# Statistics of the first rows split another way over ScalarE and VectorE, one-column matmuls alternating with q heads, and a flag read in mid FFN

## The chip, the cores and the metric

One core of one Trainium2 chip. The metric is device time in microseconds (us) of one execution. Each timed run also reports the span from the first to the last instruction and the mean granted TensorE clock, to three digits.

## The reference, cut to what matters

```python
h1 = layernorm(x) * (1 + scale_a) + shift_a      # scale, shift, gates = 6 pieces of silu(c) @ w_mod
q  = h1 @ wq                                     # 32 heads of 128
x  = x + gate_a * (windowed_attention(q, k_cache, v_cache) @ wo)
h2 = layernorm(x) * (1 + scale_b) + shift_b
out = x + gate_b * ((silu(h2 @ w_gate) * (h2 @ w_up)) @ w_down)
```

2048 rows of 1024 columns, bf16, a feed-forward network (FFN) 3584 wide. A flag, computed on the chip from bounds on q and k, selects a general attention path; with these inputs it is 0, and the general path is jumped over.

## The kernel before

Rows go in four blocks of 512. For the first block the modulation is folded into the q heads. The normalised rows are transposed into PSUM (`h0_ps`) and multiplied by 1 + scale (`hs`). Seven heads are computed from `hs`, and the shift's part of q is added later as a bias per head (`bias_q`). That bias comes out of matmuls which stream a single column: `mod_cols` computes scale and shift, 8 matmuls for each 128 of them, and `shift_cols` computes shift times wq, 28 matmuls for each half.

```python
    def stats_0(t):                      # VectorE: mean and variance of row tile t
        mv = ln[t] = sm.tile(...)
        ln_stats(t, mv)
        rstd_0(t)                        # ScalarE: 1/sqrt(variance)
    stats_0(0); act_sum(3); stats_0(1)   # act_sum, act_squares: the same statistics on ScalarE
    xpose_0(0, ln_norm(0)); warm(4)      # warm(n): n useless matmuls of 512 columns
    act_squares(3); stats_0(2); rstd_0(3, 1.0 / D)
    xpose_0(1, ln_norm(1)); warm(4)
    # ... (cut) ...
    nc.scalar.activation(out=hs[0][:, 0, :], in_=h0_ps[0][:, 0, :], ..., scale=ca1[:, 0:1])
    nc.vector.tensor_copy(out=h10[:, 0:2, :], in_=h0_ps[0][:, 0:2, :])   # rows kept for later heads
    h_scale(1)                                                           # hs from h10, on VectorE
    nc.vector.tensor_copy(out=h10[:, 2:4, :], in_=h0_ps[0][:, 2:4, :])
    h_scale(2); h_scale(3)
    # ... (cut: first halves, dt 0 to 3, of all seven heads) ...
    for g in range(4):
        q0(g, range(4, DT))              # second half of head g: 4 matmuls of 512 columns
    sa_cols(0)                           # 32 one-column matmuls (shift, first half)
    q0(4, range(4, DT))
    for dt in range(4):
        ln_mod(("h1", 0), dt, ca1, sa)
    shift_cols(0)                        # 28 one-column matmuls, then bias_q on VectorE
    sa_cols(1)                           # 32
    q0(5, range(4, DT))
    shift_cols(1)                        # 28
    q0(6, range(4, DT))
```

## Time and profile before

| | before |
|---|---|
| median of the first three runs (low to high) | 1274.93 us (1273.68 to 1275.57) |
| the profiled run, its span and mean clock | 1273.63 us, 1271.9 us, 1.000 |
| TensorE (PE) busy | 1262.7 us, 99% |
| PE idle before 31 us / from 31 us to the last matmul / after it | 3.84 / 0.18 / 5.19 us |

The prediction shows the lines that carry this: the busy times by stretch, PE's timeline of the start, the chain, and the flag's instructions at the end. One more view is needed, VectorE's timeline of the first 10 us (start us, busy us, engine, line, operation, out<-in, count, and in brackets the idle time ahead of it and what ended it). Row tile x2 had landed at 5.58, x3 at 6.24.

```profile
6.77 1.28 DVE L833 BATCH_NORM_STATS2 st<-x 128x6 f32<-128x512 bf16 x2
...
9.65 1.00 DVE L852 TENSOR_SCALAR xn<-x,mv 128x1024 bf16<-128x1024 bf16 x2 [0.95 <-ACT mv L954]
```

VectorE comes to x2 at 6.77 without a wait. The last two row tiles are normalised from 9.65 on, and what they wait for is ScalarE (ACT), which makes the statistics of x3.

### The profile page before, as it was taken

To read this page: it belongs to the slowest core of one execution; us is meant where nothing else is said; L and a number is where in the kernel's file an instruction comes from. 1 tells how busy PE (TensorE), PEld (TensorE's weight loads), DVE (VectorE), ACT (ScalarE), POOL (GpSimd) and SP (SyncE) were. 2 spreads that over 40 slices of the span, in tenths; PEclk is the share of its full clock that TensorE was granted. 3 is DMA by queue.
4 is the path that set the end of the run, shared out by engine and by line. 5 is a ranking of instruction groups with operands and counts; after the bars stand their busy time and mean duration, and the time that the engine had idled before them with its cause. 6 is when DMAs were issued, how large, how long until landed. Compare 5 with 4: busy or idle time off the path is not lost.

```text
span 1271.9 us, 18166 instructions
## 1 busy us (share of the span) xinstructions
PE 1262.7 (99%) x7587; PEld 641.2 (50%) x7587; DVE 609.0 (48%) x1335; ACT 334.9 (26%) x439; POOL 1.3 (0%) x10
## 2 busy tenths in 40 slices
PE   8999999999999999999999999999999999999998
PEld 4555555555555555555554444444444444444444
DVE  4766568977587756476664632311222112221122
ACT  3543334443343433334341111011100111011100
POOL 0000000000000000000000000000000000000000
PEclk9999999999999999999999999999999999999999
DMA  9897657768556655455575466536633565425701
GB/s 290 203 246 180 175 133 176 170 171 195 142 134 173 152 137 153 113 154 112 120 203 145 135 224 184 161 96 212 210 116 102 171 213 179 157 91 172 242 22 64
DMA packets 306844, 204.46 MB, mean 161 GB/s; under 512 B 145601, under 2 KB 303297, under 8 KB 306754
## 3 DMA queue, kind: packets, MB, share of 16 engines
q1 hardware_dynamic: 301842, 199.03, 57.7%
q10 hardware_dynamic: 4912, 4.20, 1.0%
q8 instruction: 61, 1.00, 0.3%
q14 instruction: 29, 0.24, 0.1%
HBM read 165.94 MB, written 4.21 MB: 134 GB/s over the span
## 4 chain that ended last, share of the span: by engine, by line
PE 98%; DVE 1%; DMA 0%; issue 0%; ACT 0%; ACTq 0%
PE gu_ps L1299 30%; PE a_ps L1217 17%; PE q_ps L1142 16%; PE d_ps L1319 15%; PE o_ps L1185 9%; PE s_ps L1153 9%; PE q_ps L1013 1%; DVE st L833 0%; DVE junk L1076 0%; PE mod_ps L773 0%; DMA x<-in_A_x_dram 0%; PE h_ps L948 0%; DVE qT L934 0%; DVE hT L873 0%; DVE junk L804 0%
## 5 line engine op out<-in xcount | busy, mean ns | idle before, releaser
L1155 ACT ACTIVATE pT<-s_ps 128x1024 bf16<-128x1024 f32 x256 | 249.2, 1021 | 346.8 <-PE s_ps L1153 346.8
L1217 PE MATMUL a_ps<-wo,oT 128*128 128x512 bf16 x1024 | 241.9, 379 | 0.0
L1142 PE MATMUL q_ps<-hT,wq 128*128 128x512 bf16 x968 | 229.2, 379 | 0.0
L1305 DVE TENSOR_TENSOR guT<-gu_ps,sg 128x512 bf16<-128x512 f32 x112 | 77.4, 692 | 284.4 <-ACT sg L1304 284.4
L1299 PE MATMUL gu_ps<-hT,wg 128*128 128x512 bf16 x896 | 211.7, 379 | 0.0
L1304 ACT ACTIVATE sg<-gu_ps 128x512 bf16<-128x512 f32 x112 | 66.9, 597 | 488.6 <-PE gu_ps L1299 480.1
L1319 PE MATMUL d_ps<-wd,guT 128*128 128x512 bf16 (+2 forms) x952 | 194.2, 366 | 0.0
L1299 PE MATMUL gu_ps<-hT,wu 128*128 128x512 bf16 x672 | 163.3, 379 | 0.0
L1217 PEld LDWEIGHTS <-oT 128*128 128x128 bf16 x1024 | 100.2, 98 | 120.6
L934 DVE CAST qT<-q_ps 128x512 bf16<-128x512 f32 x121 | 83.6, 691 | 147.9 <-PE q_ps L1142 147.6
L1142 PEld LDWEIGHTS <-wq 128*128 128x128 bf16 x968 | 94.7, 98 | 114.1
L1319 PEld LDWEIGHTS <-guT 128*128 128x128 bf16 x952 | 90.9, 98 | 103.0
L1185 PEld LDWEIGHTS <-pT 128*128 128x128 bf16 x2048 | 126.7, 98 | 30.8 <-issue 0.4
L1299 PEld LDWEIGHTS <-wg 128*128 128x128 bf16 x896 | 87.6, 98 | 105.5
L1185 PE MATMUL o_ps<-v_sb,pT 128*128 128x130 bf16 x2048 | 137.1, 220 | 0.1
L1153 PE MATMUL s_ps<-qT,kT 128*128 128x512 bf16 x512 | 131.9, 379 | 0.1
L1299 PEld LDWEIGHTS <-wu 128*128 128x128 bf16 x672 | 65.8, 98 | 79.3
L1172 DVE TENSOR_TENSOR oq<-o_ps,rl 128x256 bf16<-128x256 f32 (+2 forms) x256 | 100.5, 419 | 3.7
L1323 DVE TENSOR_TENSOR f<-d_ps,gb_bc 128x512 f32<-128x512 f32 (+2 forms) x34 | 22.5, 660 | 140.5 <-PE d_ps L1319 140.5
L1225 DVE TENSOR_TENSOR acc<-a_ps,acc 128x512 f32<-128x512 f32 x64 | 44.1, 689 | 37.2 <-PE a_ps L1217 37.2
L1153 PEld LDWEIGHTS <-kT 128*128 128x128 bf16 x512 | 44.9, 98 | 30.8 <-issue 0.5
L1299 PE MATMUL gu_ps<-hT,v_sb 128*128 128x512 bf16 x224 | 57.5, 379 | 0.0
(92 smaller groups left out, 420.7 us busy)
## 6 DMA issues: line engine op xcount, KB each, us to landing
wq<-in_A_wq_dram SPq DMA_DIRECT2D x64, 512.0 KB
wo<-in_A_wo_dram SPq DMA_DIRECT2D x64, 512.0 KB
wg<-in_B_w_gate_dram SPq DMA_DIRECT2D x56, 512.0 KB
wd<-in_B_w_down_dram SPq DMA_DIRECT2D x56, 512.0 KB
wu<-in_B_w_up_dram SPq DMA_DIRECT2D x42, 512.0 KB
v_sb<-in_B_w_up_dram SPq DMA_DIRECT2D x14, 512.0 KB
x<-in_A_x_dram SPq DMA_DIRECT2D x16, 256.0 KB
wm<-in_w_mod_dram SPq DMA_DIRECT2D x4, 1024.0 KB
```

The lines of the kernel that those rows point to most:

```text
L934: nc.vector.tensor_copy(out=t, in_=q_ps)
L1142: nc.tensor.matmul(q_ps, lhsT=w, rhs=hT[("h1", cc)][:, dt, :], start=(dt == 0), stop=(dt == DT - 1))
L1153: nc.tensor.matmul(s_ps[:, i, :], lhsT=kT[:, kv, j * P:(j + 1) * P], rhs=qT[g], start=True, stop=True)
L1155: nc.scalar.activation(out=p[:, 2 * jj:2 * jj + 2, :], in_=s_ps, func=ACT.Exp, scale=scale)
L1172: nc.vector.tensor_tensor(out=dst, in0=ps[:, s0:s0 + cnt, 0:Dh], in1=sc, op=ALU.mult)
L1185: nc.tensor.matmul(o_slot["ps"][:, s_, :], lhsT=pT[g][:, j, t * P:(t + 1) * P], rhs=v_sb[:, kv, j, 0:VN], start=(j == 0), stop=(j == WT - 1))
L1217: nc.tensor.matmul(a_ps, lhsT=oT[(cc, 2 * q + i)][:, hh % 4, t * P:(t + 1) * P], rhs=wo_tiles[(cc, q, dh, i)][:, hh % 4, :], start=(hh == ...
L1225: nc.vector.tensor_tensor(out=acc[(cc, t)][:, dsl], in0=a_ps, in1=acc[(cc, t)][:, dsl], op=ALU.add)
L1299: nc.tensor.matmul(ps[:, n, :], lhsT=gu_w[(cc, fg, nm, dt // 4)][:, dt % 4, fi * P:(fi + 1) * P], rhs=hT[("h2", cc)][:, dt, :], start=(dt ...
L1304: nc.scalar.activation(out=g, in_=ps[:, 0, :], func=ACT.Silu)
L1305: nc.vector.tensor_tensor(out=guT[(cc, fg)][:, fi, :], in0=ps[:, 1, :], in1=g, op=ALU.mult)
L1319: nc.tensor.matmul(d_ps, lhsT=guT[(cc, f // 4)][:, f % 4, t * P:(t + 1) * P], rhs=wd_tiles[(cc, dh, f // 4)][:, f % 4, c0:c0 + w], start=( ...
```

## The change

The intent: share the statistics so that neither engine waits for the other, scale the first row blocks straight out of PSUM on both engines, put a head between any two groups of one-column matmuls, and read the flag on each engine in the second FFN block in place of the end.

```diff
     stats_0(0)
-    act_sum(3)
-    stats_0(1)
+    act_sum(1)
+    rstd_0(0)
+    stats_0(2)
+    act_squares(1)
+    warm(3)
     xpose_0(0, ln_norm(0))
     ... (cut: warm(5), stats_0(3), xpose_0 of 1, 2 and 3)
+    h_scale(0, h0_ps[0][:, 0, :])              # VectorE, out of PSUM
     ... (cut: a modulation group)
+    h_scale(1, h0_ps[0][:, 1, :], True)        # ScalarE
     ... (cut: two modulation groups)
+    h_scale(2, h0_ps[0][:, 2, :])
+    h_scale(3, h0_ps[0][:, 3, :], True)
+    for dt in (0, 2):
+        nc.vector.tensor_copy(out=h10[:, dt:dt + 2, :], in_=h0_ps[0][:, dt:dt + 2, :])
     ... (cut)
     shift_cols(0)
+    q0(5, range(4, DT))
     sa_cols(1)
-    q0(5, range(4, DT))
+    q0(6, range(4, DT))
     shift_cols(1)
-    q0(6, range(4, DT))
     ... (cut)
     for cc in range(NTC):                      # FFN blocks
+        if cc == 1:
+            over = nc.values_load(flag[0:1, 0:1], min_val=0, max_val=1)
     ... (cut: a dependency that keeps each engine but PE from moving its read to the end)
-        over = nc.values_load(flag[0:1, 0:1], min_val=0, max_val=1)
         with tc.If(over > 0):
             general_path(tc, *args)
```

More of the change, by code (lines that the diff above doesn't have):

```diff
@@ L958, in stats_0 @@
         ln_stats(t, mv)
-        rstd_0(t)
     def act_sum(t):
@@ L973, in fast_path, with h_scale @@
     stats_0(0)
-    act_sum(3)
-    stats_0(1)
+    act_sum(1)
[3 more added lines that the diff above has]
+    warm(3)
     xpose_0(0, ln_norm(0))
-    warm(4)
-    act_squares(3)
-    stats_0(2)
-    rstd_0(3, 1.0 / D)
+    rstd_0(1, 1.0 / D)
+    rstd_0(2)
+    warm(5)
+    stats_0(3)
     xpose_0(1, ln_norm(1))
-    warm(4)
-    n2 = ln_norm(2)
+    xpose_0(2, ln_norm(2))
+    rstd_0(3)
     n3 = ln_norm(3)
     mod_cols(1, 0, ca1, True, (0,))
-    xpose_0(2, n2)
     xpose_0(3, n3)
-    mod_cols(1, 0, ca1, True, (1, 2, 3))
     hT[("h1", 0)] = h10
     hs = [blkA("hs", [P, 4, TCW]) for _ in range(DH)]
-    def h_scale(dt):
-        nc.vector.tensor_scalar(out=hs[dt // 4][:, dt % 4, :], in0=h10[:, dt, :],
-                                scalar1=ca1[:, dt:dt + 1], scalar2=None, op0=ALU.mult)
-    nc.scalar.activation(out=hs[0][:, 0, :], in_=h0_ps[0][:, 0, :], func=ACT.Identity,
-                         scale=ca1[:, 0:1])
-    nc.vector.tensor_copy(out=h10[:, 0:2, :], in_=h0_ps[0][:, 0:2, :])
-    h_scale(1)
-    nc.vector.tensor_copy(out=h10[:, 2:4, :], in_=h0_ps[0][:, 2:4, :])
-    h_scale(2)
-    h_scale(3)
+    def h_scale(dt, src=None, on_act=False):
+        src = h10[:, dt, :] if src is None else src
+        if on_act:
+            nc.scalar.activation(out=hs[dt // 4][:, dt % 4, :], in_=src, func=ACT.Identity,
+                                 scale=ca1[:, dt:dt + 1])
+        else:
+            nc.vector.tensor_scalar(out=hs[dt // 4][:, dt % 4, :], in0=src,
+                                    scalar1=ca1[:, dt:dt + 1], scalar2=None, op0=ALU.mult)
+    h_scale(0, h0_ps[0][:, 0, :])
+    mod_cols(1, 0, ca1, True, (1,))
+    h_scale(1, h0_ps[0][:, 1, :], True)
+    mod_cols(1, 0, ca1, True, (2, 3))
+    h_scale(2, h0_ps[0][:, 2, :])
+    h_scale(3, h0_ps[0][:, 3, :], True)
+    for dt in (0, 2):
+        nc.vector.tensor_copy(out=h10[:, dt:dt + 2, :], in_=h0_ps[0][:, dt:dt + 2, :])
     nc.scalar.copy(out=h10[:, 4:8, :], in_=h0_ps[1])
@@ L1348, in fast_path @@
     for cc in range(NTC):
+        if cc == 1:
+            at_load = len(nc.cur_bb.bb.instructions)
+            over = nc.values_load(flag[0:1, 0:1], min_val=0, max_val=1)
         for fg in range(NFG):
@@ L1369, in fast_path @@
     assert not tasks
+    loads = {}
+    for ins in nc.cur_bb.bb.instructions[at_load:]:
+        if ins.engine not in loads:
+            loads[ins.engine] = ins.name
+        elif loads[ins.engine] and ins.engine != mybir.EngineType.PE:
+            tc.add_manual_dep(
+                ins, loads[ins.engine],
+                mybir.DependencyInfo(mybir.DependencyClass.NoSync, mybir.DependencyReason.DATA),
+                reason="flag is read before the end")
+            loads[ins.engine] = None
+    return over
 def kernel(tc, *args):
@@ L1375 @@
         flag = gp.tile([1, 1], I32, name="flag")
-        fast_path(tc, flag, *args)
-        over = nc.values_load(flag[0:1, 0:1], min_val=0, max_val=1)
+        over = fast_path(tc, flag, *args)
         with tc.If(over > 0):
```

## The prediction

> **What bounds the kernel now.** I began with the page's busy table: TensorE (PE) is busy 1262.7 of 1271.9 us at full granted clock, so the change can only touch the 9.2 us in which it is not. The busy times by stretch say where those are.
>
> ```profile
> core 0: us, PE busy (x) PEld busy (x) DVE busy (x) ACT busy (x) POOL busy (x), PEclk, DMA share, GB/s
> 0.00:1.60 1.60, 0.00 (x1) 0.10 (x1) 0.66 (x3) 0.85 (x1) 0.70 (x6) 1.00 0.00 0
> 1.60:12.70 11.10, 9.83 (x86) 4.89 (x86) 6.90 (x16) 7.11 (x20) 0.60 (x4) 1.00 0.97 319
> 12.70:31.00 18.30, 17.33 (x213) 9.81 (x213) 7.44 (x26) 2.60 (x4) 0.00 (x0) 1.00 1.12 294
> 31.00:1266.70 1235.70, 1235.52 (x7290) 626.39 (x7287) 593.39 (x1291) 324.33 (x417) 0.00 (x0) 1.00 0.58 158
> 1266.70:1271.90 5.20, 0.00 (x0) 0.00 (x0) 0.58 (x2) 0.00 (x0) 0.00 (x0) 1.00 0.10 24
> ```
>
> From 31 us to the last matmul PE idles 0.18 us in all. What can be won lies in the first 31 us (the normalisation of the first 512 rows and the first seven q heads) and in the last 5.2 us. PE's timeline of the start then shows each of its waits:
>
> ```profile
> 11.89 0.81 PE L1013 MATMUL q_ps<-hs,wq 128*128 128x512 bf16 x3
> 13.16 0.81 PE L1013 MATMUL q_ps<-hs,wq 128*128 128x512 bf16 x3 [0.47 <-DVE hs L993]
> 14.15 3.18 PE L1013 MATMUL q_ps<-hs,wq 128*128 128x512 bf16 x14 [0.18 <-DVE hs L993]
> ...
> 23.15 0.94 PE L773 MATMUL mod_ps<-siluc,wm 128*128 128x1 bf16 x32
> ...
> 25.91 0.94 PE L773 MATMUL mod_ps<-siluc,wm 128*128 128x1 bf16 x32 [0.26 <-DVE bias_q L1027]
> ```
>
> The first heads wait for scaled rows (hs), and later a group of one-column matmuls waits until VectorE has emptied their PSUM buffer. The chain that ended last goes on from there:
>
> ```profile
> 27.73 0.69 PE sh_ps L1024 x28
> 28.43 0.02 issue
> 28.45 0.18 DVE bias_q L1029
> 28.63 0.03 issue
> 28.65 0.76 DVE qT L938
> 29.41 0.02 issue
> 29.43 0.02 ACTq L936
> 29.45 0.04 issue
> 29.50 0.70 ACT qT L936
> 30.19 0.04 issue
> 30.24 0.59 PE s_ps L1153 x2
> ```
>
> The first score matmul (s_ps) is bound by the last shift columns (sh_ps), by way of the bias add and two q evacuations in a row: 30.24 - 28.25 (the last shift column's start) = 1.99 us. From s_ps on PE is full, so the start is worth what s_ps moves.
>
> At the end, the instructions of the flag's line and of the branch's line:
>
> ```profile
> L1377 DVEq TENSOR_LOAD <-flag x1: 540/540/540, 1267.0 to 1267.0; - x1
> L1377 ACTq TENSOR_LOAD <-flag x1: 474/474/474, 1267.7 to 1267.7; - x1
> ...
> L1378 ACTq COMPARE_BRANCH  x1: 54/54/54, 1268.3 to 1268.3; - x1
> ```
>
> After that branch ScalarE's next instruction comes at 1270.90, and SyncE's closing waits end 0.05 us after it; VectorE's branch is at 1267.7 and its next instruction at 1270.7.
>
> [...] 2.6 us from branch to next instruction on ScalarE, 3.0 on VectorE. The change leaves the branches where they are. [...] the 128x1024 bf16 PSUM copy took 0.69 us, the 128x512 fp32 one 0.69 too. [...] ScalarE's first q evacuation (29.50) waits for VectorE's (to 29.40) [...]. In the built program the new scaling has such waits: row block 2 on VectorE waits for block 1 on ScalarE, block 3 on ScalarE for block 2.
>
> **The change part by part.**
>
> 1. Statistics. ScalarE takes x1, not x3; VectorE does x0, x2, x3. The x tiles land at 3.49, 4.13, 5.58 and 6.24. VectorE: stats of x0 from 3.52 (1.3 + 0.2 as now), then idle until x2 at 5.61 (before, x1 followed at 4.97); aggregate 6.92, xn0 7.05, stats of x3 7.46 to 8.98, xn1 8.90, xn2 9.36. ScalarE: sum of x1 4.65 to 5.70, rstd0 to 6.23, squares 6.36 to 7.6, rstd1 to 8.2, rstd2 to 8.6, rstd3 9.01 to 9.54. So xn3 starts at about 9.82, against 10.11 now: 0.29 us. The 0.95 us idle on VectorE in front of xn2 goes, but 0.64 us comes back as the wait for x2.
>
> 2. Scaling. Transposes of block 3 start at 10.56 (now 10.72), so hs0 can start at 10.99. On VectorE from PSUM, at the copy's rate: 0.16 + 512 x 0.52 ns = 0.43 us (estimate). Then modT1 11.38, hs1 on ScalarE 11.6 to 12.3 (0.69 each, as now), hs2 on VectorE 12.33 to 12.77, hs3 on ScalarE 12.81 to 13.5. The heads follow: hs0 at 11.64 (behind the modulation matmuls), hs1 12.34, hs2 12.98 (now 14.15), hs3 13.63 to 14.27. By that alone PE is 1.17 us early.
>
> 3. The price. The two copies out of this PSUM tile used to lie between the scalings and ended at 13.71. Now they come after hs3, 13.54 to about 14.88 (2 x 0.67). The fourteen-matmul run needs that tile for heads 0 and 1 after six matmuls, so PE waits from 14.27 to about 14.93, where it now arrives at 15.44. What is left of the 1.17 is 0.51 us. PE then comes to the shift's modulation matmuls at 22.64 in place of 23.15; their weights' last packet lands at 22.37, so no wait.
>
> 4. The reordered heads. Before, from 23.15 to the last shift column's end 28.27 is 5.12 us: two modulation groups (0.80 each), two shift groups (0.70), two heads (0.86) and the 0.40 us wait for bias_q. After, the wait goes but a third head comes ahead of the last shift group: 5.12 - 0.40 + 0.86 = 5.58. That group therefore ends at 22.64 + 5.58 = 28.22, only 0.05 us earlier, and s_ps comes 1.99 us behind its last column as now: 30.19 for 30.24. PE has less to fill that stretch with (the head moved away from it), so two waits appear there: about 0.37 us before the next head's q matmuls (they need the shift's PSUM buffer) and 0.72 us before s_ps. The two halves of the rewrite nearly cancel: -0.05 us.
>
> 5. The flag. TENSOR_LOADs of 0.54 (VectorE) and 0.47 us (ScalarE) leave the end; in the built program they stand at the second FFN block, where ScalarE and VectorE idle for microseconds between matmuls; PE's own stays at its end and was not on the path (PE is through at 1270.1). ScalarE's branch moves from 1268.28 to 1267.73, its next instruction to about 1270.35. SyncE's closing waits then run on their own, some 0.065 us each: the row that now waits at 1270.38 for VectorE goes through, and the last ends about 1270.56 for 1270.98. -0.42 us. The last store (issued 1267.36, landed about 1269.5) sets a floor under that.
>
> 6. The scheduler also moved some weight loads in front of others near the first down projection, and eight VectorE operations ahead of one eviction. The gate and up loads are issued about 20 us earlier, the down loads when their buffers come free, as now. PE has four PSUM buffers there and 6 us a tile: nothing expected.
>
> Sum: 1274.93 - 0.05 - 0.42 = 1274.46; I say 1274.4.
>
> **The rivals.** (a) The heads carry their whole 1.17 us, if the PSUM tile is free earlier than I think or the last shift group does not bind. For it: the change is meant so, and three waits of PE go. Against it: the copies are program-ordered after hs3, and the chain of 1.99 us is measured. Then 1273.3 to 1273.8. (b) [...] 0.75 us as its fp32 evictions with a scalar took. hs0 and hs2 lie in series with hs1 and hs3, 0.6 us more; the start loses about 0.55 us and the total is 1275.0. For it: no bf16 PSUM scaling by VectorE stands in this trace; against it, the copy's rate. (c) Weights bind: the modulation weights land at 22.37 and 25.30, so a start earlier by over 0.75 us would be given back. This caps (a) rather than costs. (d) The tail is held by the store alone[...]: the 0.42 us goes, 1274.9.
>
> **Range and chances.** All these lie within 1273.2 to 1275.4, which also holds the spread of the runs before (1273.68 to 1275.57) in part. 2% is 25 us; PE's work alone is 1235 us of the middle and is unchanged, so neither side of 2% has a way: 0.005 each, 0.99 within.
>
> **What would show it.** Right: xn3 at 9.8 and hs2's heads at about 13.0; a PE wait of some 0.65 us near 14.9 for the copies (step 3); no wait of PE for bias_q ahead of the second shift modulation, but two waits, of about 0.4 and 0.7 us, after the last shift group (step 4); s_ps at 30.1 to 30.3; no TENSOR_LOAD of ScalarE or VectorE after 840 us, and 4.8 us for 5.2 from the last matmul to the end. Wrong: s_ps before 29.8 or after 30.6, a VectorE scaling row of 0.7 us, a tail as long as before, or a PE wait between 31 us and the last matmul that was not there.

Rival (b) says that VectorE's scaling of a row block out of PSUM takes 0.75 us. The 0.43 us of step 2 was an estimate: the copy of 1024 columns out of PSUM took 0.69 us and a 4-column operation out of PSUM (modT) 0.16, so (0.69 - 0.16) / 1024 = 0.52 ns a column.

## The result, and the profile after

| | before | after |
|---|---|---|
| median, first comparison (6 runs each) | 1275.01 us (1273.68 to 1277.67) | 1274.16 us (1273.45 to 1274.44) |
| median, a later chip (9 and 5 runs) | 1276.05 us (1274.11 to 1278.30) | 1273.82 us (1273.68 to 1274.39) |
| first profile: span, clock | 1271.9 us, 1.000 | 1272.5 us, 0.999 |
| first score matmul (s_ps) | 30.24 | 30.77 |
| last matmul to the end | 5.19 us | 4.78 us |

Ratios here are the mean time of one kernel's fast runs over that of the other's in the same rounds, so they are not quite the ratios of these medians. The first comparison gave 0.9990 (95% interval 0.9977 to 1.0003), the later one 0.9986 (0.9973 to 1.0000): the same within 2%.

Two things are odd. The medians are better by 0.85 and 2.2 us, yet the first profile of the changed kernel is 0.6 us longer than the first of before. And the kernel before scatters over 4 us, the changed one over 1.

VectorE's timeline of the changed kernel at the start; x2 landed at 6.16, x3 at 6.84:

```profile
6.18 1.29 DVE L833 BATCH_NORM_STATS2 st<-x 128x6 f32<-128x512 bf16 x2 [1.16 <-DMA x<-in_A_x_dram]
...
9.48 1.42 DVE L852 TENSOR_SCALAR xn<-x,mv 128x1024 bf16<-128x1024 bf16 x3
```

The 0.95 us of waiting for ScalarE are gone, and x2 is waited for as it lands. PE's timeline from there (142 matmul records are missing from this trace, so some x4 read x3):

```profile
15.49 1.90 PE L1019 MATMUL q_ps<-hs,wq 128*128 128x512 bf16 x8 [0.47 <-DVE hT L1008]
...
25.58 1.02 PE L1019 MATMUL q_ps<-hs,wq 128*128 128x512 bf16 x4
26.44 0.94 PE L773 MATMUL mod_ps<-siluc,wm 128*128 128x1 bf16 x32
27.46 0.81 PE L1019 MATMUL q_ps<-hs,wq 128*128 128x512 bf16 x3
28.10 0.84 PE L1030 MATMUL sh_ps<-sa_bf,wq 128*128 128x1 bf16 x28
29.20 1.02 PE L1148 MATMUL q_ps<-hT,wq 128*128 128x512 bf16 x4 [0.26 <-DVE bias_q L1035]
30.77 0.59 PE L1159 MATMUL s_ps<-qT,kT 128*128 128x512 bf16 x2 [0.54 <-ACT qT L936]
```

These are the waits of steps 3 and 4 as predicted, though each is shorter: one for the copies, none for bias_q ahead of the modulation group at 26.44, and two behind the last shift group. All of it lies 0.56 to 0.58 us later than predicted, and x2 landed 0.58 us later.

The flag's instructions, and those of the branch's line (duration in ns as min/median/max, then first and last start):

```profile
L1357 DVEq TENSOR_LOAD <-flag x1: 547/547/547, 833.2 to 833.2; - x1
L1357 ACTq TENSOR_LOAD <-flag x1: 472/472/472, 834.3 to 834.3; - x1
```

```profile
L1397 ACTq COMPARE_BRANCH  x1: 54/54/54, 1268.7 to 1268.7; - x1
...
L1397 ACTq EVENT_SEMAPHORE  x1: 17/17/17, 1271.4 to 1271.4; - x1
```

The two reads are out of the end, which is 0.41 us shorter. ScalarE's next instruction still comes 2.66 us after its branch.

### The profile page after: what moved, and what is told of

Its sections match the earlier page's. It is cut to its first block, busy times and chain, and to the rows that moved or that the text cites. A ratio compares the mean times of both kernels' runs of the same rounds, so it can differ in the third digit from the quotient of the medians.

```text
span 1272.5 us, 18029 instructions
## 1 busy us (share of the span) xinstructions
PE 1254.6 (99%) x7445; PEld 640.9 (50%) x7587; DVE 608.9 (48%) x1335; ACT 335.3 (26%) x440; POOL 1.3 (0%) x10
## 4 chain that ended last, share of the span: by engine, by line
PE 96%; DVE 1%; DMA 1%; issue 1%; ACT 0%; SPq 0%; DVEq 0%; ACTq 0%
PE gu_ps L1305 29%; PE a_ps L1223 17%; PE q_ps L1148 16%; PE d_ps L1325 15%; PE o_ps L1191 9%; PE s_ps L1159 8%; DMA hT<-xn 1%; PE q_ps L1019 1%; DMA x<-in_A_x_dram 0%; DVE junk L1082 0%; PE mod_ps L773 0%; DVE st L833 0%; DVE xn L852 0%; ACT hs L995 0%; PE sh_ps L1030 0%
```

## The experiments

First theory: the end gives 0.4 us, the start nothing. Rival: the start gives the gain. Every kernel gave correct results, each was timed in five rounds beside the kernel before.

**e1: the flag's part alone.** The kernel before with only the last hunks of the diff.

> The kernel before with nothing but the flag's read moved into the second FFN block. My theory (the flag is worth 0.42 us at the end, the new start about nothing): from the end of the last matmul to the end 4.8 us for 5.2 before; the first score matmul (s_ps) at 30.2, as in the kernel before, if x2 lands at any time up to 6.7; time 0.4 us under the kernel before, ratio 0.9997, inside its interval. Rival (the start carries the gain and the closing part is held by the store): 5.2 us at the end, time as before. In the middle, no new wait of PE over 0.1 us if the wait of 0.31 us at 770 us in the changed kernel is DMA chance; the same wait again if the flag's read in the FFN brings it.

Median 1274.75 us, before 1274.82, ratio 1.0002 (0.9989 to 1.0016). The end took 4.85 us, as I expected. No wait at 770 us, so the flag's read does not bring that one. But s_ps came at 31.63 instead of 30.2. PE's timeline has no new wait:

```profile
25.91 0.94 PE L773 MATMUL mod_ps<-siluc,wm 128*128 128x1 bf16 x32 [0.26 <-DVE bias_q L1027]
26.71 1.02 PE L1013 MATMUL q_ps<-hs,wq 128*128 128x512 bf16 x4
27.57 0.84 PE L1024 MATMUL sh_ps<-sa_bf,wq 128*128 128x1 bf16 x28
28.27 1.86 PE L1013 MATMUL q_ps<-hs,wq 128*128 128x512 bf16 x4
29.92 1.91 PE L1142 MATMUL q_ps<-hT,wq 128*128 128x512 bf16 x4
31.63 0.65 PE L1153 MATMUL s_ps<-qT,kT 128*128 128x512 bf16 x2
```

The head at 28.27 takes 1.86 us where the same four matmuls took 1.02 at 26.71. The busy times by stretch say why (last columns: granted clock, DMA share, GB/s):

```profile
core 0: us, PE busy (x) PEld busy (x) DVE busy (x) ACT busy (x) POOL busy (x), PEclk, DMA share, GB/s
...
24.30:28.30 4.00, 3.74 (x97) 2.95 (x95) 1.87 (x8) 0.00 (x0) 0.00 (x0) 1.00 0.85 177
28.30:31.70 3.40, 3.40 (x14) 1.21 (x11) 3.21 (x8) 1.34 (x2) 0.00 (x0) 0.50 0.84 227
31.70:34.10 2.40, 2.40 (x13) 1.10 (x12) 2.12 (x4) 1.78 (x2) 0.00 (x0) 0.99 0.63 219
```

For 3.4 us TensorE ran at half clock. The trace's clock record has it from 28.32 to 31.73, 3413 ns, and stretches between two changes of the clock in other traces are multiples of that: 1266.345 us at full clock in those of before and after is 371 times, e5's 6.83 us at half clock (27.20 to 34.03) twice. So I reckon in windows of 3413 ns on a grid. The grid starts elsewhere in each execution: the record of full clock begins at 4.43 us here, at 4.46 in the trace of after, at 5.59 in that of before. The page's row of the clock in 40 slices, 32 us each, shows 9 throughout and hides it. The changed kernel, with its grid at almost the same place (from 4.46), kept its clock:

```profile
28.30:31.70 3.40, 2.60 (x35) 1.42 (x33) 2.68 (x7) 1.65 (x3) 0.00 (x0) 1.00 0.90 276
```

**e2: the start alone.** The changed kernel with the flag read at the end.

> The changed kernel with the flag's read back at the end, so the new start alone. My theory: s_ps at 30.19 + (landing of x2 - 5.58), so 30.2 where x2 lands at 5.58 and 30.77 where it lands at 6.16; VectorE idles 0.64 to 1.2 us ahead of the statistics of x2; 5.2 us from the last matmul to the end; time within 0.6 us of the kernel before, on either side. Rival (the start carries the whole difference of the medians, 0.85 us, or the 1.17 us of hs2's heads): s_ps at 29.4 or under, time 0.8 us or more under the kernel before.

1274.28 us, ratio 0.9995 (0.9982 to 1.0009). x2 landed at 5.67 and s_ps came at 30.28, the formula to the hundredth. The end took 5.19 us. PE has a wait of 0.14 us at 770 us here too, without the flag's part.

**e3: the third head back behind the last shift group, parts of heads between.**

> The changed kernel with the one-column matmuls laid between parts of two heads, and the third head after the last shift group as in the kernel before. My theory (step 4: the third head ahead of the last shift group costs 0.86 us and the bias_q wait can be had away with 0.43 us of other work): no PE wait for bias_q, none of the two waits after the last shift group (0.26 and 0.54 us), s_ps 0.80 us earlier than the changed kernel at the same landing of x2, so 29.4 for 5.58 and 29.97 for 6.16; time 0.8 us under the changed kernel. Rival (the waits after the last shift group stand for a bound of their own on VectorE or ScalarE, not for the order): s_ps unchanged to 0.2 us, a wait of the same size elsewhere.

```diff
     sa_cols(0)
-    q0(4, range(4, DT))
+    q0(4, (4, 5, 6))
     ...
     shift_cols(0)
-    q0(5, range(4, DT))
+    q0(4, (7,)); q0(5, (4,))
     sa_cols(1)
-    q0(6, range(4, DT))
+    q0(5, (5, 6, 7))
     shift_cols(1)
+    q0(6, range(4, DT))
```

Median 1274.14 us, ratio 0.9993 (0.9980 to 1.0007). The waits for bias_q and behind the last shift group went, as expected, and yet s_ps came at 31.75, where 30.22 was expected for this x2 (6.41). Its clock record shows half clock from 28.35 to 31.76.

**e4: no copies out of PSUM.** The two `tensor_copy` are taken out; the same rows are formed later as `hs` plus shift.

> The changed kernel without the two copies of row blocks out of PSUM after the scaling: the same rows are formed later from the scaled ones by adding the shift, so the result is rounded once more. My theory (step 3, the copies hold the PSUM tile): the PE wait of 0.47 us near 15.5 goes, heads 0 and 1 follow without a wait, and the shift's modulation matmuls start 0.47 us earlier at the same landing of x2, but not ahead of the landing of their weights (22.2 to 22.4 us); s_ps earlier by the same 0.3 to 0.5 us. Rival (the tile is held by ScalarE's scaling of block 3 or by ScalarE's copy, not by VectorE's two copies): a wait of at least 0.3 us stays there, s_ps unchanged.

Median 1273.44 us, ratio 0.9987 (0.9974 to 1.0001). The wait near 15.5 went and none took its place. The shift's modulation group began at 23.10, where the changed kernel would be at 23.73 for this x2 (6.68): 0.63 us, somewhat more than the 0.47 of the wait. s_ps came at 30.65, also 0.64 us ahead of the changed kernel's formula, where 0.3 to 0.5 was expected. The copies did hold the tile.

**The theory after these four.** No wait of PE explains e1: in the window ahead of the slow one none was longer than 0.26 us. The changed kernel had waits of 0.47 and 0.54 us (at 15.49 and 30.77) and kept a clock of 1.00 up to 34.10. What was short in e1 is streaming. Of the window before the slow one, 24.91 to 28.32, four wide matmuls (of 512 columns) fill 0.86 us (0.215 us from one start to the next); the rest went to one-column matmuls, which PE's busy time counts as busy (3.74 of the 4.00 us from 24.30 to 28.30). I counted the streaming share so in every window of the first traces, transposes by their 128 columns. The two that were followed by half clock had 0.26 (e1) and 0.31 (e3). Those not followed by it had 0.36 and more; the profile of before had 0.39 at the least, in a grid that lay better. Moving the grid over the profile of before, a third to a half of all places leave some window under that, by whether 0.31 or 0.36 is taken; moving it over the head groups of the changed kernel, none does (least share 0.44). A theory from a few windows of these traces, no more; why the share should matter is not shown.

A run without a profile has only its mean clock. One half window (a window at half clock) takes 1.71 of 1272 us, 0.0013; the half clock at the end took 0.0007 in the trace of after (from 1270.80 on). The three profiles in which I found half windows before the end (e1, e3, e5) read 0.998, 0.998 and 0.996, the other eleven 0.999 or 1.000. So I take it that 1.000 means no such window, 0.998 or less at least one, and 0.999 leaves it open. The next runs were chosen to make such windows, and to take them away.

**e5: all one-column groups together**, and the three heads behind them; else the kernel before.

> The kernel before with all four groups of one-column matmuls one after the other and the three heads behind them. New theory, from the traces of the flag-only and split-heads kernels: the clock of TensorE is granted by windows of 3.41 us, and a window follows at half clock when in the one before it matmuls streamed columns for less than about a third of the time (0.26 and 0.31 were followed by one, 0.36 and more never)[...]. Here about 4 us lie together, so by the phase of the windows 84% of the executions should get a window of half clock: at least 4 of 5 runs with a mean clock of 0.999 or less, most at 0.998, one such window in the profile near 24 to 31 us, s_ps at 30.7 without it and 32.2 with it, time 1 to 1.5 us over the kernel before. Rival (the half-clock windows come by chance or from outside the core, whatever the order of the matmuls): as often as in the kernel before, some 4 in 10, time 0.5 us over the kernel before from the waits alone.

Median 1277.21 us for 1276.19, ratio 1.0013 (0.9999 to 1.0027); the means differ by 1.56. Clocks 0.996, 0.998, 0.999, 0.998, 0.998. In the profile there are two half windows in a row, 27.20 to 34.03, behind a window without any wide matmul, and s_ps came at 34.12:

```profile
28.30:31.70 3.40, 3.40 (x13) 1.19 (x11) 3.26 (x9) 1.05 (x2) 0.00 (x0) 0.50 0.86 270
31.70:34.10 2.40, 2.40 (x7) 0.84 (x6) 2.40 (x6) 0.30 (x1) 0.00 (x0) 0.52 0.36 122
```

Why the second window was slow too (its predecessor streamed 0.37 of the time at full-clock rates) I did not settle. The slow windows of e1 and e3 streamed 0.50 and more by the same count, and full clock came back behind them (0.99 in the mean of 31.70 to 34.10, in both); no run here tests where the difference comes from.

**e7: the head order alone**, on the kernel before.

> The kernel before with only the head order of the changed kernel. Theory of the windows: no window of half clock in any of the five runs (lowest share of streaming in any window 0.44, for any phase), so no run at a clock of 0.998 or less; s_ps at 30.24 + 0.455 = 30.7, as step 4 of the prediction has it; slowest of the five runs under 1274.9 us, mean 0.1 to 0.3 us under the kernel before. Rival (windows by chance): runs at 0.998 as in the kernel before, 4 in 10, mean 0.45 us over the kernel before.

No run at 0.998 or less; the kernel before had six of nine. s_ps came at 31.39; x3 had landed 0.68 later than in the first profile of before, which leaves 31.39 - 30.24 - 0.68 = 0.47 us for the order, 0.46 predicted (5.58 - 5.12 in step 4). Median 1275.37, mean 1275.26 against 1275.84 for before, so 0.58 us under where I had said 0.1 to 0.3, and its slowest run was 1275.80, over my bound of 1274.9; I had reckoned with fewer half windows in the kernel before and with x landing as in the first profile.

**e8: the changed kernel with the old head order.**

> The changed kernel with the head order of the kernel before. Theory of the windows: some 4 in 10 runs with a window of half clock, which cost 1.4 us each; without it s_ps 0.45 us earlier than in the changed kernel at the same landing of x2, so 29.74 + (landing of x2 - 5.58); the fastest runs 0.4 us under the fastest of the changed kernel (1273.45), the slowest 1 us over its slowest (1274.44). Rival (the order is worth 0.45 us and nothing else): all runs 0.45 us under those of the changed kernel.

Clocks 0.999, 0.999, 0.999, 0.998, 0.997: the half windows are back. Without one, in the profile, s_ps came at 30.03 (30.04 expected for x2 at 5.88). The slowest run took 1275.76, 1.3 us over the slowest of the changed kernel, the fastest 1273.39, only 0.06 under its fastest instead of 0.4. Median 1274.58, ratio 0.9993 (0.9979 to 1.0007).

**e6: the statistics of x2 on ScalarE, of x1 on VectorE.**

> The changed kernel with the statistics of x2 on ScalarE and those of x1 on VectorE, so that VectorE has no wait for a late tile between x0 and x1. Theory (the start of the changed kernel follows the landing of x2 one for one): the last rows are normalised from landing + 3.9 us, 9.5 where x2 lands at 5.58 and 10.0 at 6.16, 0.3 us earlier than in the changed kernel; s_ps earlier by the same 0.3 us, and not by the whole wait, as ScalarE's sums now follow x2. Rival (VectorE's own work is the bound and x2's landing is not): xn3 no earlier than in the changed kernel at the same landing.

A miss in what it won. Normalising the last rows began at 9.49 for x2 at 5.42, 0.13 ahead of the changed kernel's rule below, but s_ps came at 30.19, later than that rule's 30.03, and at 32.5 PE waited 1.25 us for weights of the next heads. Median 1274.40, ratio 0.9988 (0.9974 to 1.0001); no run at 0.998 or less.

**e10: the kernel before with three useless matmuls.**

```diff
     shift_cols(0)
+    for i in range(3):
+        nc.tensor.matmul(q0_ps[5], lhsT=zero_w, rhs=hs[0][:, i, :], start=False, stop=False)
     sa_cols(1)
```

> The kernel before, nothing reordered, with three useless matmuls of 512 columns (weights of zero, added into a head's sum) between the first shift group and the second modulation group. Theory of the windows: streaming in the emptiest window goes from 0.25 to 0.44, so no run at a clock of 0.998 or less, although the program has more to do; s_ps 0.24 to 0.4 us later than in the kernel before without a half-clock window, 30.24 + (landing of x3 - 6.24) + 0.3; mean 0.2 us or more under the kernel before. Rival (windows by chance, or set off by what lies on other engines): runs at 0.998 as often as in the kernel before, mean 0.3 us over it. If zeros do not count as streaming, the windows stay too; the profile then shows one at a phase at which the kernel before has one.

This is the clearest of the runs: nothing reordered, and work added. No run at 0.998 or less, where the kernel before had six of nine; median 1274.64 us for 1276.05, mean 1274.72 for 1275.96. The interval of the ratio just reaches 1 (0.9992, 0.9978 to 1.0005), so it is the clocks that decide here, not the time. The profile, in PE's timeline and in the stretch that was slow in e1:

```profile
25.69 0.81 PE L1058 MATMUL q_ps<-hs,zero_w 128*128 128x512 bf16 x3
...
30.66 0.59 PE L1157 MATMUL s_ps<-qT,kT 128*128 128x512 bf16 x2
```

```profile
28.30:31.70 3.40, 3.33 (x35) 1.66 (x32) 2.79 (x8) 1.75 (x3) 0.00 (x0) 1.00 0.87 242
```

That stretch alone proves little, since the grid lies elsewhere here than in e1. In its own grid, the window ahead of it is 25.27 to 28.69. Seven wide matmuls lie in it (the record of one is missing) and stream 0.44 of the time; without the three of zero weights it would be 0.25, less than in e1, and yet full clock followed. So by this count the three matmuls with weights of zero did what other wide ones did: full clock (1.00) behind a share of 0.44. Five runs are few: if each had the 15 in 27 of the kernel before, none would come out in some 2% of such sets.

**e11: the changed kernel again.**

> The changed kernel once more, to count windows on one chip with the others. Theory of the windows: no run at 0.998 or less, s_ps at 30.19 + (landing of x2 - 5.58), 4.8 us from the last matmul to the end; mean 1 us under the kernel before, of which 0.4 from the end, 0.5 from the windows and the rest from the start. Rival (windows by chance): as many runs at 0.998 as in the kernel before.

No run at 0.998 or less. x2 landed at 6.01 and s_ps came at 30.62, the formula again; the end took 4.87 us. Mean 1273.97 us, 1.99 under the kernel before. I had said 1: the kernel before had more half windows than I reckoned with.

**e9: the fourth head between.** The changed kernel, with another set of heads between the groups:

```diff
-    for g in range(4):
+    for g in range(3):
         q0(g, range(4, DT))
     sa_cols(0)
-    q0(4, range(4, DT))
+    q0(3, range(4, DT))
     ...
     shift_cols(0)
-    q0(5, range(4, DT))
+    q0(4, range(4, DT))
     sa_cols(1)
-    q0(6, range(4, DT))
+    q0(5, range(4, DT))
     shift_cols(1)
+    q0(6, range(4, DT))
```

> The changed kernel with the second half of the fourth head moved behind the first group of one-column matmuls, and the seventh head back behind the last one: each group has a head behind it, and no head is taken from behind the last. Theory of the windows: streaming fills at least 0.45 of any window, so no run at 0.998 or less; none of the two PE waits after the last shift group; s_ps at 29.9 + (landing of x2 - 5.58), 0.3 us ahead of the changed kernel at the same landing, if the weights of the first group have landed by 22.3; time 0.3 us under the changed kernel. Rival (windows by chance): runs at 0.998 in 3 or 4 of 10. Rival for the size: the modulation weights land later than the groups now start (22.3 and 25.5), a wait for them appears and s_ps is no earlier.

No run at 0.998 or less; neither of the two waits; s_ps at 29.43 for x2 at 5.46, 0.64 us ahead of the rule of the changed kernel. But median 1274.69, slower than e11. PE's timeline shows one place where it went in the profiled run:

```profile
31.16 0.59 PE L1160 MATMUL s_ps<-qT,kT 128*128 128x512 bf16 x2
33.80 0.39 PE L1149 MATMUL q_ps<-hT,wq 128*128 128x512 bf16 x1 [2.05 <-DMA wq<-in_A_wq_dram]
```

The next q weights landed at 33.76 (in the two profiles of the changed kernel at 31.99 and 32.40). Whether the earlier start brings that or chance, these runs don't tell.

**e12: the fourth head between, without the copies.** e4 and e9 together.

> The kernel of the fourth head between, without the two copies out of PSUM. Theory: the wait for the copies goes, so the start no longer loses what a late x2 brings up to 0.5 us; s_ps at the later of 29.9 and 29.9 + (landing of x2 - 5.58) - 0.47, bound by the landing of the modulation weights (22.2 to 22.5) plus 7.55; no run at 0.998 from the head groups, though a late x2 leaves a window of little streaming in the statistics as well; the fastest of the kernels run, 1273.0 median. Rival (the weights' landing moves with the start, so nothing is won): s_ps as in the fourth head between.

The fastest: median 1273.07 us (1272.63 to 1274.52), ratio to before 0.9977 (0.9964 to 0.9991), and four of its five runs are under every run of the changed kernel in the same call; no run at 0.998 or less. The profiled run was its slowest, one with late weights:

```profile
20.16 2.33 PE L1017 MATMUL q_ps<-hs,wq 128*128 128x512 bf16 x10 [0.77 <-DMA wq<-in_A_wq_dram]
23.17 0.95 PE L773 MATMUL mod_ps<-siluc,wm 128*128 128x1 bf16 x32 [0.68 <-DMA wm<-in_w_mod_dram]
```

Its modulation weights landed at 23.12; adding 7.55 gives 30.67, and s_ps came at 30.74. In this run the start is bound by loads, no longer by engines.

## Why the prediction was right, and what it left out

The time was right: 1274.4 predicted, 1274.16 measured, and the later runs of the changed kernel lie in the range too. The steps hold when the kernels are compared at the same landings and without half windows.

| profile | x2 / x3 landed | last rows normalised from | s_ps |
|---|---|---|---|
| before | 5.58 / 6.24 | 10.11 = x3 + 3.87 | 30.24 = x3 + 24.00 |
| e7 (start of before, new order) | 6.23 / 6.92 | 10.80 = x3 + 3.88 | 31.39 = x3 + 24.47 |
| after | 6.16 / 6.84 | 10.36 = x2 + 4.20 | 30.77 = x2 + 24.61 |
| e2 | 5.67 / 7.06 | 9.87 = x2 + 4.20 | 30.28 = x2 + 24.61 |
| e11 | 6.01 / 6.67 | 10.21 = x2 + 4.20 | 30.62 = x2 + 24.61 |

Step 1 (statistics): right, with a part I had not seen. The old start follows the landing of x3 one for one, the new one that of x2. Where x3 comes 0.66 us behind x2, as in the profile of before, the change is worth 0.05 us (24.66 - 24.61), the prediction's own number; where x3 is 1.39 behind, as in e2, it is worth 0.78. Over the fourteen profiles the mean distance was 0.85, so 0.24 us.

By the prediction's own sign, s_ps at 30.77 was "wrong"; the table shows that this profile had x2 late, and that the kernel before would have been as late.

Step 2 (scaling): VectorE's scaling out of PSUM took 0.48 us for the estimate of 0.43, so rival (b) falls. Step 3 (the price): the copies held PE for 0.47 us (0.65 predicted), and e4 shows that nothing else did. Step 4 (order): 0.47 us by e7, and by e8 the other way, for 0.46; the two waits were 0.26 and 0.54 for 0.37 and 0.72. Step 5 (flag): 0.41 us for 0.42 in the first profile, 0.34 in e1 without the start. The nine profiles with the early read end 4.84 us behind the last matmul in the mean, the five with the late one 5.20, so it is worth about 0.35. Step 6: the wait of 0.31 us in mid FFN in the first profile was on the list of what would be wrong. It is there in e10, which has the old start and the old flag (0.11 us), is longest in e4 (0.38), and is absent in e1, so the flag does not make it. In the first profile VectorE there waits for a DMA transpose until 768.89 (767.37 in that of before). Why that one is late in some executions stays open.

No step failed; a term was missing. The prediction's first sentence, that the change can only touch the 9.2 us in which PE is not busy, left it out: a half window lies in PE's busy time (e1: 3.40 of 3.40 us busy at a clock of 0.50). I took the clock as full because the one profile of before showed it full, and the spread of the runs before for noise. That profile was the fastest of the runs then known. Of the 27 later runs of the kernel before, ten had a clock of 1.000 and took 1274.18 us in the mean; eight at 0.998 took 1275.74, six at 0.996 took 1277.49, one at 0.997 took 1276.21, two at 0.999 lie between. The steps of 1.6 and 1.8 us fit one half window each: a window of 3413 ns at a clock of 0.50 loses 1.71 us of work. Of 46 runs of kernels with a head, or useless matmuls, between the shift group and the next modulation group (the changed kernel, e2, e4, e6, e7, e9 to e12) none was at 0.998 or less; of 42 with the old spacing or e3's half heads (before, e1, e3, e8) 20 were. Some may be missed: 26 of the 46 read 0.999, and the slowest of these in e2 took 1275.73 us, 1.4 over the next.

So step 4 had the order's cost right and its sign wrong. On the chip of the last call the kernel before took 1275.96 us in the mean, and 1274.41 in its three runs at full clock. By this the half windows cost it 1.55 us a run, and the new order gives that back for 0.47 us of waits, which are in the start's 0.24. With 0.24 from the start and 0.35 from the end this makes 2.14 us; 1.99 was measured, though the interval of the ratio (0.9973 to 1.0000) holds anything from 0 to 3.4. Against the three runs at full clock alone the change wins 0.44 us; the predicted -0.05 - 0.42 is that size. So the number owes something to luck: it was counted from a median of three runs, 1274.93. From the 1276.05 the same steps would give 1275.6, above the range, where 1273.82 was measured. The first theory, that the end is all of it, is not refuted by e1's time (its interval holds the 0.4 us) but by the half windows; its rival goes too, as the balance over the engines is the small part.

What stays open: in which windows the unprofiled runs were slow, why six runs of the kernel before lost two windows' worth, and whether a bound lies between 0.31 and 0.36 at all.

## What to carry to other kernels

PE's busy share did not show the lost clock here: in e1 PE was busy for 3.40 of 3.40 us at a granted clock of 0.50. Where matmuls of one column lie together, look at the granted clock, count the columns streamed, and try wide matmuls between, useless ones if there are no others: with three of them none of e10's five runs was at 0.998 or less, against six of nine of the kernel before (the gain in time alone is within the noise). Where one kernel's runs scatter by a fixed step, look at the granted clock of each run, and zoom into the profile before averaging the step away. Compare starts of two kernels at the same landing of the loads that they hang on.
